# A decode kernel whose loads run on 16 DMA engines: part of one V unit moved to loads of 32 partitions, and the first K half issued ahead of wq

## The chip, the cores and the metric

One core of one Trainium2 chip runs the kernel. The metric is the device time of one execution in microseconds; quoted are medians of several executions. PE is the engine for matmuls (PEld its weight loads), DVE, ACT and POOL the vector, scalar and GpSimd engines, SP the one that issues the loads. SBUF is the memory on the chip that the loads fill, in tiles of 128 partitions; a DMA engine moves a load from HBM into it in packets, here one row of a partition or part of it each (the trace of the kernel before has 1920 packets of 16,384 bytes, 128 for each of the 15 units that are loaded whole). A ratio of two kernels is computed as the mean time of one kernel's fast runs over that of the other's in the same rounds, so it is not quite the ratio of the medians quoted beside it.

## The reference

A decode step for two tokens: layer norm, then attention over the last 2048 keys of a cache (32 query heads on 16 KV heads of 128), plus an MLP with squared ReLU, both added to the input. All tensors are bf16.

```python
xn = _layernorm(x)                                   # x: [2, 1, 576]
# attention: q = xn @ wq, window W = 2048 of 8192 keys, 16 KV heads, softmax, @ wo
# MLP: h = relu(xn @ w1 + b1) ** 2 ; h @ w2 + b2      (576 -> 4608 -> 576)
return x + attention(xn, k_cache, v_cache, wq, wo) + mlp(xn, w1, b1, w2, b2)
```

What matters for the time is that 53.6 MB of K, V and weights are read from HBM once, and little is computed on each byte.

## The kernel before

K and V come in eight units each (u = 0 to 7): 2 MB, a tile of 128 partitions with 16,384 bytes in each. A unit holds four heads of one batch; partition c*4 + h holds 64 keys of head h. V units and their pieces are written as `[c, h, bytes]`, c being the slowest dimension.

```python
TH = 4; CP = P // TH              # 4 heads x 32 chunks of 64 keys = 128 partitions
def unit_view(cache, u):
    tq, b = divmod(u, B)
    return cache[b, tq*TH:(tq+1)*TH, S0:Sk, :].rearrange("h (c j) d -> c h (j d)", c=CP)

def issue_kv(tiles, cache, u, name, parts=1):
    tl = kvpool.tile([P, UE], BF16, tag="kv", name=f"{name}_{u}")     # 6 buffers
    v = unit_view(cache, u); n = UE // parts; tiles[u] = tl
    return [lambda i=i: nc.sync.dma_start(out=tl[:, i*n:(i+1)*n], in_=v[:, :, i*n:(i+1)*n])
            for i in range(parts)]
# ... start: wq chunk 0, K half 0, wq chunk 1, K half 1, the rest of wq, then K1, w1, V0, ...
def load_v(u):
    for f in issue_kv(v_tiles, A_v_cache, u, "v"):
        f()
# ... end: w2 in five pieces, one after the other; out_ps gathers all products
W2P = [(0, 0, 9), (0, 9, 18), (1, 0, 9), (1, 9, 15), (1, 15, 18)]
```

Every large load covers 128 partitions. They are all issued on one queue (SP), most of them some 15 to 30 us before they land (medians of 13.0 to 29.4 us by the page, 6.9 for wq).

## Time and profile before

| | before |
|---|---|
| time | 137.48 us median of 3 |
| read from HBM | 53.6 MB, about 425 GB/s in the steady part |
| DMA engines | 90% busy or more in slices 2 to 38 of 40 |
| PE busy | 76% of the span, with waits for K units |
| last w2 piece complete | 132.26 us of a span of 135.6 |

Lines of the page of the kernel before: in the DMA line each digit is the busy share of one fortieth of the span (9 is 90% or more), below it what was moved; then a queue, and the shares of the chain of waits.

```profile
DMA  5999999999999999999999999999999999999940
GB/s 112 418 419 418 428 442 402 420 429 440 430 393 430 438 411 409 444 425 396 440 440 406 445 420 425 404 443 423 425 430 413 430 415 426 422 410 417 393 166 1
q8 instruction: 16, 0.26, 0.8%
DMA 55%; PE 35%; DVE 3%; issue 2%; POOL 1%; ACT 1%; SPq 1%; POOLq 0%; ACTq 0%
```

The rate stays at 393 to 445 GB/s in slices 2 to 38: the DMA engines do not run out of loads. The end of the chain of waits of the kernel before, in order of time (start, duration, what):

```profile
119.21 13.05 DMA w<-in_B_w_dram
132.26 0.04 issue
132.30 0.55 PE out_ps L213 x6
132.85 0.02 issue
132.87 0.45 DVE fin_sb L414
```

The last link is a load. PE's wait for K in the kernel before (in total, times, longest) has slack behind it, so PE is not what bounds the time:

```profile
PE kT_ps L237 <- DMA k<-in_A_k_cache_dram: 9.9, 4, 4.3
```

A load over 128 partitions adds to its semaphore (a counter on which other engines wait) 16 times, and PE goes on after the last: at 132.30 us, after 132.26. With 16 packets under way (in the trace of the kernel before exactly 16 at 216 of 236 moments, one every 0.5 us from 10 to 128 us), one increment is read here as one engine's. These 16 increments for the last w2 piece, in us, as the event records of the trace have them:

```
128.90 128.97 129.03 129.10 129.19 129.24 129.66 129.88
132.11 132.13 132.14 132.15 132.18 132.21 132.25 132.26
```

Eight engines are done about 3 us before the other eight, although the 128 packets of the piece all have 3456 bytes. The 16 packets of the instruction queue (q8), 16 KB each, tell why. They go with PE's program: 16 for some 4110 rows (the trace has 4108 weight loads and matmuls), and 8 for 2126 rows in fewer_pe_instructions below. The first of these fetches, at 16.75 us, took 1.06 us, an 8 KB data packet that starts as it ends took 0.81 us for 0.31, and from then on one increment of each load is about 1.45 us behind (25.87 us in K unit 1, whose other 15 come by 24.41). After eight fetches eight are; the ninth, at 79.6 us, puts one engine about 3 us behind (84.69 us in K unit 5, whose first seven increments come by 81.70).

### The profile page before, as it was taken

How to read it: one execution, taken by the hardware profiler on the slowest of the kernel's cores; microseconds unless marked ns; L12 is line 12 of the kernel's file. 1: busy time of each engine (PE TensorE's matmuls, PEld its weight loads, DVE VectorE, ACT ScalarE, POOL GpSimd, SP SyncE). 2: the span in 40 equal slices, each digit the busy share in tenths (PEclk: the TensorE clock that was granted, in tenths of full speed). 3: DMA queues.
4: the chain of work that ended last, by engine and by line, in shares of the span. 5: the costliest groups of instructions: out<-in, count | busy, mean ns of one | idle time of the engine just before them, and what ended most of it. 6: DMA issues, size and time to landing. Idle time of an engine off the chain costs nothing.

```text
span 135.6 us, 4461 instructions
## 1 busy us (share of the span) xinstructions
PE 102.5 (76%) x2054; PEld 91.9 (68%) x2054; DVE 53.9 (40%) x124; ACT 43.0 (32%) x47; POOL 10.0 (7%) x31
## 2 busy tenths in 40 slices
PE   1049947599968999879943993999399599768961
PEld 0039947589968999839933993688399479664530
DVE  7502421574352325422653446355634645660001
ACT  6705550165012521004701550272155127110000
POOL 6400000110110001100011001101100110110000
PEclk9999985569855685556985698698559959955599
DMA  5999999999999999999999999999999999999940
GB/s 112 418 419 418 428 442 402 420 429 440 430 393 430 438 411 409 444 425 396 440 440 406 445 420 425 404 443 423 425 430 413 430 415 426 422 410 417 393 166 1
DMA packets 5278, 53.90 MB, mean 397 GB/s; under 512 B 630, under 2 KB 652, under 8 KB 1164
## 3 DMA queue, kind: packets, MB, share of 16 engines
q1 hardware_dynamic: 5188, 53.61, 94.7%
q8 instruction: 16, 0.26, 0.8%
q0 software_dynamic: 64, 0.01, 0.0%
q14 instruction: 2, 0.02, 0.0%
q10 hardware_dynamic: 8, 0.00, 0.0%
HBM read 53.62 MB, written 0.00 MB: 395 GB/s over the span
## 4 chain that ended last, share of the span: by engine, by line
DMA 55%; PE 35%; DVE 3%; issue 2%; POOL 1%; ACT 1%; SPq 1%; POOLq 0%; ACTq 0%
DMA k<-in_A_k_cache_dram 41%; PE kT_ps L237 18%; DMA w<-in_B_w_dram 10%; PE hT_ps L323 5%; DMA b_sb<-in_B_b_dram 4%; PE sc_ps L252 4%; PE out_ps L213 4%; PE oT_ps L289 3%; PE qT_ps L225 1%; ACT kT L240 1%; POOL b_sb L146 1%; DVE l L271 1%; DVE sub L266 1%; SPq L94 0%; DVE fin_sb L414 0%
## 5 line engine op out<-in xcount | busy, mean ns | idle before, releaser
L237 PE MATMUL kT_ps<-ident,k 128*128 128x128 bf16 x512 | 47.3, 260 | 9.9 <-DMA k<-in_A_k_cache_dram 9.9
L237 PEld LDWEIGHTS <-k 128*128 128x128 bf16 x512 | 39.6, 119 | 11.8 <-DMA k<-in_A_k_cache_dram 10.7
L240 ACT COPY kT<-kT_ps 128x1024 bf16<-128x1024 bf16 x32 | 32.3, 1012 | 40.1 <-PE kT_ps L237 40.0
L242 DVE COPY kT<-kT_ps 128x1024 bf16<-128x1024 bf16 x32 | 22.0, 690 | 33.4 <-PE kT_ps L237 33.4
L252 PE MATMUL sc_ps<-qT_all,kT 128*128 128x8 bf16 x512 | 21.6, 168 | 1.6 <-ACT kT L240 0.8
L252 PEld LDWEIGHTS <-kT 128*128 128x128 bf16 x512 | 19.1, 100 | 2.6 <-ACT kT L240 1.2
L289 PE MATMUL oT_ps<-pT,v 128*128 128x8 bf16 x512 | 15.5, 167 | 1.9 <-issue 1.4
L269 ACT ACTIVATE pT<-sub 128x512 bf16<-128x512 f32 x8 | 5.0, 630 | 35.1 <-DVE sub L266 35.1
L289 PEld LDWEIGHTS <-v 128*128 128x128 bf16 x512 | 14.4, 99 | 2.1 <-issue 1.6
L271 DVE TENSOR_REDUCE l<-pT 128x8 f32<-128x512 bf16 x8 | 8.5, 1066 | 4.2 <-ACT pT L269 4.2
L213 PE MATMUL out_ps<-wo,ws 128*2 128x288 bf16 x64 | 8.3, 438 | 2.4 <-DVE ws L309 2.4
L323 PE MATMUL hT_ps<-xnT,w 128*128 128x2 bf16 x144 | 9.8, 201 | 0.0
L323 PEld LDWEIGHTS <-w 128*128 128x128 bf16 x144 | 9.4, 165 | 0.0
L258 DVE TENSOR_REDUCE m<-sc_ps 128x8 f32<-128x512 f32 x8 | 5.5, 692 | 9.7 <-PE sc_ps L252 9.7
L262 POOL PARTITION_ALL_REDUCE gmax<-m x8 | 2.9, 364 | 84.8 <-DVE m L260 84.8
L213 PE MATMUL out_ps<-w,hT_sb 128*2 128x288 bf16 x72 | 6.9, 353 | 1.3 <-DMA w<-in_B_w_dram 1.3
L213 PEld LDWEIGHTS <-ws 128*2 128x2 bf16 x64 | 3.5, 115 | 5.4 <-DVE ws L309 2.8
L213 PEld LDWEIGHTS <-hT_sb 128*2 128x2 bf16 x72 | 3.8, 103 | 4.3 <-issue 1.9
L266 DVE TENSOR_TENSOR sub<-sc_ps,gm 128x512 f32<-128x512 f32 x8 | 5.5, 692 | 0.3
L225 PE MATMUL qT_ps<-xnT,wq 128*128 128x2 bf16 x128 | 4.0, 165 | 2.2 <-DMA wq<-in_A_wq_dram 1.9
L225 PEld LDWEIGHTS <-wq 128*128 128x128 bf16 x128 | 3.9, 103 | 2.2 <-DMA wq<-in_A_wq_dram 2.0
L273 POOL PARTITION_ALL_REDUCE lsum<-l x8 | 3.2, 398 | 24.5 <-DVE l L271 24.5
(58 smaller groups left out, 35.1 us busy)
## 6 DMA issues: line engine op xcount, KB each, us to landing
v<-in_A_v_cache_dram SPq DMA_DIRECT2D x8, 2048.0 KB, 28.4
k<-in_A_k_cache_dram SPq DMA_DIRECT2D x7, 2048.0 KB, 29.4
w<-in_B_w_dram SPq DMA_DIRECT2D x4, 1152.0 KB, 17.7
wo<-in_A_wo_dram SPq DMA_DIRECT2D x4, 1152.0 KB, 27.4
wq<-in_A_wq_dram SPq DMA_DIRECT2D x4, 1024.0 KB, 6.9
w<-in_B_w_dram SPq DMA_DIRECT2D x3, 1296.0 KB, 22.7
k<-in_A_k_cache_dram SPq DMA_DIRECT2D x2, 1024.0 KB, 9.1
w<-in_B_w_dram SPq DMA_DIRECT2D x1, 864.0 KB, 15.7
```

The costliest lines, as they stand in the source:

```text
L213: nc.tensor.matmul(out_ps[32 * i:32 * i + B, :], lhsT=lhsT, rhs=rhs_of(i * OH, (i + 1) * OH), start=start, stop=stop, skip_group_check=True)
L225: nc.tensor.matmul(qT_ps[:, h, :], lhsT=lhsT, rhs=xnT[:, xc, :], start=(c == 0 and h == 0), stop=(c == KC - 1), skip_group_check=True)
L237: nc.tensor.transpose(out=kT_ps[:, i * P:(i + 1) * P], in_=k_sb[:, j * Dh:(j + 1) * Dh], identity=ident[:])
L240: nc.scalar.copy(out=kT[:], in_=kT_ps[:])
L242: nc.vector.tensor_copy(out=kT[:], in_=kT_ps[:])
L252: nc.tensor.matmul(sc_ps[:, g * JG + i, :], lhsT=kT[:, i * P:(i + 1) * P], rhs=qT_all[:, b, tq * NC:(tq + 1) * NC], start=True, stop=True)
L258: nc.vector.tensor_reduce(out=m1[:], in_=sc_ps[:].rearrange("p j c -> p c j"), axis=AX.X, op=ALU.max)
L266: nc.vector.tensor_tensor(out=sub[:], in0=sc_ps[:], in1=gm2[:].unsqueeze(1).to_broadcast([P, NJ, NC]), op=ALU.subtract)
L269: nc.scalar.activation(out=pT[:], in_=sub[:], func=ACT.Exp, scale=scale)
L271: nc.vector.tensor_reduce(out=l1[:], in_=pT[:].rearrange("p j c -> p c j"), axis=AX.X, op=ALU.add)
L289: nc.tensor.matmul(oT_ps[:], lhsT=v_sb[:, j * Dh:(j + 1) * Dh], rhs=pT_tiles[u][:, j, :], start=(j == 0), stop=(j == NJ - 1))
L323: nc.tensor.matmul(hT_ps[:, s * FR + r, :], lhsT=lhsT, rhs=xnT[:, xc, :], start=(c == 0 and s == 0 and r == 0), stop=(c == KC - 1), skip_g ...
```

## The change

The intent: give eight engines more of V unit 4 and eight less, so that all end together; and have K in earlier at the start.

```diff
     k0 = issue_kv(k_tiles, A_k_cache, 0, "k", parts=2)
+    k0[0]()
     issue_wq(0)
-    k0[0]()
+    k0[1]()
     issue_wq(1)
-    k0[1]()
...
+    SK = 43
+    SKU = NU // 2
     def load_v(u):
-        for f in issue_kv(v_tiles, A_v_cache, u, "v"):
-            f()
+        if u != SKU:
+            ...                                  # as before
+        tl = kvpool.tile([P, UE], BF16, tag="kv", name=f"v_{u}")
+        v_tiles[u] = tl
+        v = unit_view(A_v_cache, u)
+        e = (NJ - SK) * Dh                       # 5376 bytes of each partition
+        nc.sync.dma_start(out=tl[:, 0:e], in_=v[:, :, 0:e])
+        for c0, c1 in ((0, 16), (16, 24), (24, 32)):       # 11008 bytes of each
+            nc.sync.dma_start(out=tl[c0 * TH:c1 * TH, e:UE], in_=v[c0:c1, :, e:UE])
```

(Two dead statements also go.) So 64 partitions go in one piece and twice 32 in two pieces. In the trace of the changed kernel the piece of 64 partitions has 16 increments (85.72 to 92.32 us). Each piece of 32 has one increment about 1.2 us after its issue starts and eight more over the transfer (88.76 to 93.31 us for the first, 92.06 to 96.63 for the second), so it is taken to run on eight engines. "Lower", "low" or "lowest" below are the engines that carry loads of fewer than 64 partitions, "upper" the others. These are names only: no record numbers an engine or says which partitions it writes.

More of the change, by code (lines that the diff above doesn't have):

```diff
@@ L343, in load_k @@
             f()
+    SK = 43
+    SKU = NU // 2
     def load_v(u):
-        for f in issue_kv(v_tiles, A_v_cache, u, "v"):
-            f()
+        if u != SKU:
+            for f in issue_kv(v_tiles, A_v_cache, u, "v"):
+                f()
+            return
+        tl = kvpool.tile([P, UE], BF16, tag="kv", name=f"v_{u}")
[5 more added lines that the diff above has]
+            nc.sync.dma_start(out=tl[c0 * TH:c1 * TH, e:UE], in_=v[c0:c1, :, e:UE])
     W2P = [(0, 0, 9), (0, 9, 18), (1, 0, 9), (1, 9, 15), (1, 15, 18)]
@@ L360 @@
     load_k(3)
-    nxt = {0: [], 1: [], 2: [lambda: load_v(2), lambda: load_k(4)]}
     def step(u, extra=()):
@@ L404 @@
                 load_k(u + 2)
-        if u >= NU - 1:
-            pass
         if u == NU - 1:
```

## The prediction

> **What bounds the kernel.** The transfers. The page shows the 16 DMA engines at 90% busy or more in slices 2 to 38 of 40, 53.6 MB at about 425 GB/s; PE is busy 76% and idles before several K units (4.3 us before unit 5, 2.3 us before unit 6, in the timeline). The chain of waits is 55% DMA, and its last link is the landing of the last w2 piece (132.26 us), then six matmuls (0.53), one copy (0.45) and the output store.
>
> **Why engines could be unequal.** Every large transfer gives 16 engines the same bytes: 53.6 MB / 16 = 3.35 MB each, at 16 KB per 0.61 us. But the increments of the last w2 piece's completion (landing events in the trace) come in two groups: eight at 128.9 to 129.9 us, eight at 132.1 to 132.3. The packet records show why: 16 instruction packets of 16 KB, one about every 7.5 us. The first takes 1.06 us, and the next data packet on that engine 0.81 instead of 0.31; after it one landing is 1.45 us behind, after the second two, after the eighth eight; the ninth puts one engine about 3 us behind. So eight engines each serve two fetches and end about 2.7 us late, and each load waits for the slowest.
>
> **What the change does.** [...] The 32-partition pieces have eight chunks in front[...]. Of V unit 4, 64 partitions x 11,008 B (705 KB) move there: eight engines carry 44 KB more, the others 44 KB less, 1.64 us each way at 26.8 GB/s. Three issues are added (0.33 to 0.55 us each on SP, which issues over 20 us ahead) and 64 to 128 packets' overhead: under 0.1 us.
>
> If the late engines are the upper eight (records carry no engine number, so this is assumed from the intent), ends become: formerly early 128.9 to 129.9 plus 1.7 = 130.6 to 131.6; formerly late 132.2 minus 1.6 = 130.6. The last landing moves from 132.26 to between 130.8 and 131.6: 0.7 to 1.5 us saved. PE can follow: the K unit 6 landing that starts its final chain moves too, and PE idles 2.3 us before it.
>
> The K half ahead of wq: nothing. In PE order its transposes come behind the matmul on b2, which waits until 8.29 us; total bytes are equal, and PE is idle later anyway.
>
> **Risk.** [...] The three pieces each write one half, with other engines' work on it at once. [...] If the late engines are the lower eight, the time rises by 1.6 us (139)[...]. No trace here shows either.
>
> **Predicted: 136.5 us, range 135.7 to 138.0; faster by over 2%: 0.04, within: 0.92, slower: 0.04.**
>
> **Right if** the last piece's 16 increments lie within 1.2 us of one another (3.3 before), K unit 6 and everything behind it completes 0.7 to 1.5 us earlier, completions before V unit 4 hardly move, instruction fetches stay at 16, packet times of V unit 4 stay at 26 GB/s. **Wrong if** packets of V unit 4 or its neighbours stretch[...], if the two groups spread to 6 us (wrong half), or if the time falls over 2%: then the first K half mattered, seen as unit 0 work starting before 8 us.

## The result

The changed kernel took 145.08 us (median of 4, 144.94 to 146.17; a fifth execution of 144.48 us, which the ratio counts in), the kernel before 137.53 (median of 4): ratio 1.0555, 95% interval 1.05 to 1.061. It is slower by 5.5%, far outside the range. The profiled execution is the slowest of them, 146.17 us.

The same lines of the page of the changed kernel:

```profile
DMA  4999999999999999999999999999999999999600
GB/s 135 371 428 421 423 446 415 414 449 423 405 426 433 428 408 422 432 406 435 423 428 437 399 266 222 225 336 417 432 423 425 423 419 430 409 417 410 266 36 1
q8 instruction: 16, 0.26, 0.8%
DMA 72%; PE 20%; issue 1%; ACT 1%; DVE 1%; POOL 1%; SPq 1%; POOLq 0%; ACTq 0%
```

Nearly all of the loss is in one place. In four slices of 3.6 us the rate falls to 266, 222, 225 and 336 GB/s, while the busy line still shows nines: the page counts a DMA engine as busy while a packet is under way, however slowly (a DMA share of 1.00 at 219 GB/s from 88 to 92 us). Before and after that stretch the rate is the old one. The end of the chain of waits of the changed kernel:

```profile
125.71 14.80 DMA w<-in_B_w_dram
140.51 0.04 issue
140.55 0.55 PE out_ps L213 x6
141.10 0.02 issue
141.12 0.45 DVE fin_sb L423
```

It ends in the same way, 8.25 us later. And PE's waits in the changed kernel (how long in total, how often, the longest) follow the transfers: 14.1 us for K where it was 9.9, and a wait of its matmuls for V, for which before only one weight load waited, 0.6 us:

```profile
PE kT_ps L237 <- DMA k<-in_A_k_cache_dram: 14.1, 4, 6.0
PE oT_ps L289 <- DMA v<-in_A_v_cache_dram: 5.3, 2, 3.1
```

Packets of the trace say more. One of the 11,008-byte packets of V unit 4 takes 0.80 us at the median; the fastest take 0.42. They run from 82.5 to 95.5 us, 13 us in all. The increments of the last w2 piece:

```
133.45 133.51 135.09 135.72 136.12 136.14 136.16 136.28
136.35 136.37 136.77 136.81 136.88 137.76 139.28 140.51
```

They are spread over 7 us, for 3.4 before. So two things went wrong: throughput was lost, and the engines ended less equal than before. The second would delay the end even without the first, since the last engine counts.

### The profile page after: what moved, and what is told of

The parts are those of the page before. It is cut to its first block, busy times and chain, and to the rows that moved or that the text cites. A ratio compares the mean times of both kernels' runs of the same rounds, so it can differ in the third digit from the quotient of the medians.

```text
span 144.1 us, 4466 instructions
## 1 busy us (share of the span) xinstructions
PE 101.8 (71%) x2054; PEld 91.2 (63%) x2054; DVE 53.7 (37%) x124; ACT 43.0 (30%) x47; POOL 10.0 (7%) x31
## 4 chain that ended last, share of the span: by engine, by line
DMA 72%; PE 20%; issue 1%; ACT 1%; DVE 1%; POOL 1%; SPq 1%; POOLq 0%; ACTq 0%
DMA k<-in_A_k_cache_dram 58%; PE kT_ps L237 12%; DMA w<-in_B_w_dram 10%; DMA b_sb<-in_B_b_dram 4%; PE oT_ps L289 2%; PE sc_ps L252 2%; PE out_ps L213 2%; ACT kT L240 1%; PE qT_ps L225 1%; POOL b_sb L146 1%; DVE sub L266 0%; SPq L94 0%; DVE fin_sb L423 0%; POOL gmax L262 0%; SPq L100 0%
## 5 line engine op out<-in xcount | busy, mean ns | idle before, releaser
L237 PE MATMUL kT_ps<-ident,k 128*128 128x128 bf16 x512 | 47.8, 259 | 14.3 <-DMA k<-in_A_k_cache_dram 14.1
L213 PE MATMUL out_ps<-w,hT_sb 128*2 128x288 bf16 x72 | 6.4, 336 | 1.7 <-DMA w<-in_B_w_dram 1.7
```

The costliest lines, as they stand in the source:

```text
L213: nc.tensor.matmul(out_ps[32 * i:32 * i + B, :], lhsT=lhsT, rhs=rhs_of(i * OH, (i + 1) * OH), start=start, stop=stop, skip_group_check=True)
L237: nc.tensor.transpose(out=kT_ps[:, i * P:(i + 1) * P], in_=k_sb[:, j * Dh:(j + 1) * Dh], identity=ident[:])
```

## The experiments

Fifteen kernels ran. The first theory, P: the pieces write one half of the partitions at a time, and engines that write the same place slow each other. The mechanism was the author's assumption; no trace shows it. Rivals: the order at the start (O), the row sizes (R), the loads on eight engines as such (E). Edits are against the kernel before unless said otherwise; medians of the kernel before in the same rounds were 137.3 to 137.5 us.

### Each part of the change alone

`order_only` has the first hunk of the diff, `split_only` the second.

> Only the K half moves ahead of wq; V unit 4 loads as before. Theory P (the loss comes from the V pieces that write one half of the partitions[...]): the same as before within 0.4% (137.0 to 138.1 us). Rival O (the order costs part of the 7.6 us): 138.5 us or more.

> Only the pieces of V unit 4; the order of before. Theory P: all of the loss, 144.5 to 146 us. Rival O: clearly under 144 us.

Measured: order_only 137.60 us, ratio 1.0026 (1.0012 to 1.0041); split_only 145.64 us, ratio 1.0615 (1.058 to 1.065). The order is worth nothing, or 0.3% to the bad; the split is the whole loss. Three stretches of split_only show it (bounds and length in us, busy us of PE, PEld, DVE, ACT and POOL with their counts, then PE's clock, the DMA share and GB/s):

```profile
84.00:88.00 4.00, 3.41 (x30) 2.29 (x31) 1.80 (x4) 0.90 (x2) 0.40 (x1) 0.50 1.01 217
88.00:92.00 4.00, 4.00 (x76) 4.00 (x75) 1.77 (x3) 2.73 (x3) 0.00 (x0) 0.75 1.02 212
92.00:96.00 4.00, 2.05 (x65) 1.92 (x62) 2.28 (x6) 1.04 (x2) 0.36 (x1) 1.00 0.98 244
```

`columns_only` keeps the cut of the rows and drops the cut of the partitions:

```diff
-        for c0, c1 in ((0, 16), (16, 24), (24, 32)):
-            nc.sync.dma_start(out=tl[c0 * TH:c1 * TH, e:UE], in_=v[c0:c1, :, e:UE])
+        nc.sync.dma_start(out=tl[:, e:UE], in_=v[:, :, e:UE])      # 128 partitions
```

> V unit 4 in two loads of 5376 and 11008 bytes a row, both over all 128 partitions and 16 engines. Theory P: the same as before, 137.3 to 138.0 us, with packets of 11008 bytes near 0.42 us. Rival R (rows that are no power of two, or their HBM addresses, are slow): 140 us or more, with these packets near 0.7 us as in the changed kernel.

Measured: 137.40 us, ratio 1.0015 (0.9994 to 1.0036), packets of 11,008 bytes at 0.418 us. R falls, and 128 packets more hardly show (137.40 us for 137.36).

### No load on eight engines, yet slow

`halves_16_engines`: the pieces are `((0, 16), (16, 32))`, so 64 partitions each.

> The 11008-byte rows in two loads of 64 partitions (0 to 63, 64 to 127), each on 16 engines: no load on eight engines, and each engine moves the bytes of before. Theory P: [...]1.6 to 3.3 us lost: 139 to 141 us, with 11008-byte packets well over 0.42 us. Rival E (the loss comes from loads on eight engines, which overload the wrong eight): the same as before, 137.5 us.

Measured: 142.30 us, ratio 1.0346 (1.032 to 1.037), packets at 0.82 us, and the same stretches:

```profile
84.00:88.00 4.00, 3.64 (x37) 2.51 (x38) 1.62 (x5) 1.13 (x2) 0.40 (x1) 0.57 1.02 217
88.00:92.00 4.00, 3.81 (x93) 3.60 (x91) 2.04 (x3) 3.07 (x4) 0.00 (x0) 1.00 0.97 220
92.00:96.00 4.00, 2.41 (x89) 2.25 (x84) 2.41 (x5) 0.85 (x2) 0.36 (x1) 0.78 1.03 427
```

E falls as the whole cause; but the loss, 4.9 us, is over the 1.6 to 3.3 that P allowed.

`eight_own_half`: the mirrored pieces `((16, 32), (0, 8), (8, 16))`. The pieces of 32 partitions now go into partitions 0 to 63. P's number takes only the piece of 64 partitions to be slow; this was the author's assumption.

> The pieces of V unit 4 mirrored: partitions 64 to 127 in one load on 16 engines, partitions 0 to 31 and 32 to 63 on eight engines each, so that the eight engines move as many bytes as in the changed kernel[...]. Theory P: [...]about half of the 4.9 us that two such pieces cost: 138.5 to 140.5 us. Rival E (the overloaded eight engines cost the time, whatever they write): near the changed kernel, 144 us or more.

Measured: 142.81 us, ratio 1.040 (1.038 to 1.043). It beats the changed kernel, but misses what P said by over 2 us. Something in P is mis-sized; "Why the prediction was wrong" adds this run up.

### Which engines are late, and what does the place written cost

From here on the loads of the kernel stay as they were. Extra loads are added behind V unit 4 into a tile that nobody reads, all from the same addresses; only the partitions differ.

```diff
     def load_v(u):
         for f in issue_kv(v_tiles, A_v_cache, u, "v"):
             f()
+        if u == NU // 2:
+            v = unit_view(A_v_cache, u)
+            for p0 in (0, 32):                       # extra_low_x2; (0,) and (64, 96) in two others
+                nc.sync.dma_start(out=spare[p0:p0 + 32, :], in_=v[0:8, :, 0:XE])   # 11008 bytes
```

> The kernel before with one more load ahead of V unit 4's successors: 352 KB into partitions 0 to 31 of a tile that nobody reads, on eight engines, 44 KB or 1.64 us for each. If these eight are the early ones (2.4 to 3.3 us of slack at the end): no change, within 0.3%. If they are the late ones: 1.6 us more, 139 us.

> Two such loads, into partitions 0 to 31 and 32 to 63: 705 KB, 88 KB or 3.3 us for each of eight engines[...]. If they are the early ones: 0.1 to 1.2 us more than before (the slack is just used up). If the late ones: 3.3 us more, 140.7 us.

> The same two loads, from the same addresses[...], but into partitions 64 to 95 and 96 to 127. Theory P: [...]both groups lose 3.3 us or more: 141 to 144 us. Rival E (engines alone count): the same as with partitions 0 to 63 within 0.3%.

Measured: extra_low 138.97 us, ratio 1.0112 (1.010 to 1.013); extra_low_x2 140.98, 1.0269 (1.025 to 1.029); extra_high_x2 145.66, 1.0623 (1.058 to 1.067).

**The low eight are not simply early, nor simply late.** The increments of the last w2 piece in extra_low_x2:

```
128.90 129.68
131.99 131.99 132.01 132.06 132.10 132.19 132.20 132.23 132.37 132.65 132.85 133.30
135.07 135.17
```

Eight engines carry about 3.3 us more, and eight are about 3 us late by fetches. If these were the same eight, eight would stand near 129 and eight near 135.5; if they were the other eight, all would stand near 132.3. There are 2, 12 and 2: two engines have neither burden, twelve have one, two have both (12 + 2 x 2 = 16). So six of the eight late engines are outside the loaded eight, and two are inside. Those two make the time longer, by 1.6 us for 44 KB (extra_low) and 3.6 us for 88 KB. In extra_low the same reading would give 2, 6, 6 and 2 increments near 129, 130.7, 132.2 and 133.8, and they stand so: the last two at 133.55 and 133.90 us. By time alone both runs pass for the answer "late" (139 and 140.7 us); only the count of increments shows that two engines make it.

**The place written matters more.** The same bytes, in loads of the same shape, cost 3.6 us in partitions 0 to 63 and 8.3 us in 64 to 127. Two stretches of extra_low_x2:

```profile
88.00:92.00 4.00, 4.00 (x85) 3.96 (x84) 1.97 (x3) 2.44 (x4) 0.00 (x0) 0.83 1.03 433
92.00:96.00 4.00, 2.74 (x94) 2.51 (x90) 2.48 (x6) 0.85 (x2) 0.37 (x1) 1.00 1.00 420
```

And of extra_high_x2:

```profile
88.00:92.00 4.00, 4.00 (x84) 3.97 (x83) 1.99 (x3) 2.79 (x3) 0.00 (x0) 0.84 1.02 212
92.00:96.00 4.00, 3.06 (x104) 2.87 (x100) 2.31 (x6) 1.01 (x1) 0.36 (x1) 1.00 0.96 244
```

From 88 to 92 us the DMA share is the same (1.03 and 1.02) and the rate is half (433 and 212 GB/s). But P, with which only engines that write the same place slow each other, does not explain the packets: at 94.5 us only two of the extra packets are still under way, 14 engines are back at ordinary rows, and all 16 packets take nearly twice their time (9216-byte rows 0.64 to 0.73 us for 0.35). That gave a new theory, L: a few such writes hold back all 16 engines.

### Few engines

Loads of 16 or 8 partitions instead of 32 (`v[0:4]`, `v[0:2]`) run on four or two engines, 88 KB on each: of the eight increments of the last w2 piece that stood near 129 us, extra_low_4 leaves four there and extra_low_2 six.

> Two extra loads of 16 partitions each (0 to 15, 32 to 47), which four engines carry, 88 KB or 3.3 us each[...]. The earlier runs say that two of the eight late engines are among the lowest eight. If none of the two is among the lowest four: 137.3 to 138.2 us, with no increment of the last w2 piece over 0.8 us later than before. If one or two are: 140.5 to 141 us, with as many increments near 135.5 us.

> The same two loads into partitions 64 to 79 and 96 to 111[...]. Theory P[...]: eight engines slow, the other eight not; the rate falls to about 320 GB/s, never near 210. Theory L ([...]since in the run with eight engines the rate stayed near 210 GB/s when only two of the pieces' packets were left): the rate falls to near 210 GB/s, and most packets take twice their time, for 6.5 us or more; then 141 to 145 us.

> As with four engines, but 8 partitions each (0 to 7, 32 to 39), on two engines. None of the late ones among the lowest two: 137.2 to 138.0 us. One or two: 140.5 us and as many increments near 135.5 us.

> As with two engines, but into partitions 64 to 71 and 96 to 103[...], 177 KB in all. Theory P: four of 16 engines slow, rate about 370 GB/s, none of the other packets slow; about 140.5 us, since a late engine can be one of the four. Theory L: near 210 GB/s for 6.5 us or more, all packets slow; 140.5 to 144 us.

| run | partitions | engines, KB in all | us | ratio (95%) |
|---|---|---|---|---|
| extra_low_4 | 0-15, 32-47 | 4, 352 | 138.93 | 1.0104 (1.009 to 1.012) |
| extra_high_4 | 64-79, 96-111 | 4, 352 | 142.91 | 1.0394 (1.037 to 1.042) |
| extra_low_2 | 0-7, 32-39 | 2, 176 | 138.54 | 1.0075 (1.006 to 1.009) |
| extra_high_2 | 64-71, 96-103 | 2, 176 | 141.87 | 1.0319 (1.030 to 1.034) |

L holds for these places. The same stretches for extra_low_2, then for extra_high_2:

```profile
88.00:92.00 4.00, 4.00 (x71) 4.00 (x69) 1.38 (x2) 2.59 (x3) 0.00 (x0) 0.65 1.02 433
92.00:96.00 4.00, 3.71 (x119) 3.51 (x116) 2.28 (x5) 1.46 (x2) 0.36 (x1) 1.00 1.03 434
```

```profile
88.00:92.00 4.00, 4.00 (x91) 3.96 (x89) 1.73 (x3) 2.59 (x3) 0.00 (x0) 0.86 1.03 209
92.00:96.00 4.00, 2.48 (x89) 2.25 (x85) 2.48 (x6) 0.86 (x2) 0.37 (x1) 0.99 1.00 387
```

With P about 370 GB/s were expected; measured is 209. All 16 packets under way at 88 us, as bytes and duration in ns:

```
extra_low_2   9216: 347 347 348 348 348 348 348 348 348 348 348 355   11008: 413 413
              16384: 612 1091
extra_high_2  9216: 705 718 719 727 729 734   11008: 838 875
              16384: 1255 1271 1273 1274 1276 1281 1285 1444
```

And the number of engines that do it matters little: with two the loss is 4.4 us, with four 5.5. Read from the packets of each microsecond from 78 to 100 us, what was moved less than 425 GB/s adds up to 3.3, 3.5 and 4.6 us with two, four and eight engines (extra_high_x2), though the bytes double each time. The rest of the 8.3 us of extra_high_x2 is about what the same extra bytes cost in extra_low_x2, 3.6 us. The low runs miss what was expected (138.5 and 138.9 us for at most 138.0 and 138.2; in extra_low_4 the last increment is 1.15 us later than before, at 133.41 us, for at most 0.8). The extra bytes take more than the 3 us of slack that early engines have (88 KB at 16 KB in 0.61 us, as packets of the kernel before took, are 3.3 us, an estimate); that those engines are the last ones is assumed. No increment of either run stands near 135.5, and four and six stand near 129, so none of the four engines, and neither of the two, is late. If the four are among the eight that carry loads of 32 partitions, which is not shown, the two late ones of these are in the other four.

### The same two halves, at other partitions

Two loads of 8 partitions again, `p0 in (4, 36)` in extra_next_2: in partitions 0 to 63 as in extra_low_2, but four further on. Then `(72, 104)` in extra_cross_next_2: in 64 to 127 as in extra_high_2, but eight further on. For the first, one of two outcomes was expected, that of extra_high_2 or that of extra_low_2; for the second, that of extra_high_2 or about 400 GB/s with few slow packets.

> The two extra loads on two engines once more, but into partitions 4 to 11 and 36 to 43[...]. [...]the rate falls to near 210 GB/s for about 6.5 us, packets take twice their time, 141.5 to 142.2 us as with partitions 64 to 71. [...]no fall of the rate, 138.5 us as with partitions 0 to 7.

> The two extra loads on two engines, into partitions 72 to 79 and 104 to 111[...]. [...]near 210 GB/s for 6.5 us, all packets at twice their time, about 141.9 us. [...]

Measured: extra_next_2 141.45 us, ratio 1.0298 (1.028 to 1.032); extra_cross_next_2 141.97 us, ratio 1.0322 (1.030 to 1.035). The times are nearly equal, the ways to them are not. The stretch from 88 to 92 us of extra_next_2, and of extra_cross_next_2:

```profile
88.00:92.00 4.00, 4.00 (x93) 3.96 (x90) 1.73 (x4) 2.70 (x3) 0.00 (x0) 0.88 1.02 404
```

```profile
88.00:92.00 4.00, 4.00 (x79) 3.96 (x77) 1.81 (x3) 2.98 (x3) 0.00 (x0) 0.82 1.00 201
```

In extra_next_2 the rate falls by about a sixteenth (404 GB/s for 433 in extra_low_2). Of the packets at 88 us one of 9216 bytes takes 0.68 us and one of 11,008 takes 0.83, and the rest take their usual time. One increment of the last piece comes at 136.12 us and all others by 132.41: a single engine makes that time. That fits two engines that slow each other, as theory P has it; that they write the same place is not shown. So neither of the two outcomes came out whole. At 4 to 11 and 36 to 43 two packets of the 16 were slow, at 64 to 71 and 72 to 79 with their counterparts 32 further on the rate of all halved (209 and 201 GB/s). Why all engines slow down there is not shown.

### Are the fetches the reason that engines are late?

`fewer_pe_instructions` loads the same bytes and leaves out half of PE's program. Its output is wrong, which doesn't matter for the time. (The check did not notice what is left out.)

```diff
-        for i in range(JG):                          # scores: eight matmuls
-            nc.tensor.matmul(sc_ps[:, g * JG + i, :], lhsT=kT[:, i * P:(i + 1) * P], rhs=q, ...)
+        nc.tensor.matmul(sc_ps[:, g * JG:(g + 1) * JG, :], lhsT=kT[:, 0:P], rhs=q_broadcast, ...)
...                                                   # P V: one matmul of eight; q: two chunks of five
```

> Wrong on purpose: the loads of before, byte for byte, but half of the PE instructions (2126 rows for 4110; most P V and score matmuls left out). If instruction fetches make eight engines late: 7 or 8 fetches of 16 KB for 16, the late engines behind by one step (1.45 us) for two, the last w2 landing near 130.8 us for 132.26, and 135.5 to 136.4 us. If the late engines are slow of themselves: both groups 3 us apart as before, and within 0.4% of 137.4 us.

Measured: 136.03 us, ratio 0.9906 (0.989 to 0.992). Its line for the instruction queue:

```profile
q8 instruction: 8, 0.13, 0.4%
```

The increments of the last w2 piece are 128.88 to 129.98 (eight) and 130.41 to 130.78 (eight): the late eight are one step behind, not two. So the fetches make the lateness, and the second one on each engine costs this kernel 1.3 us. PE also did less in this run, but the span ends 3.3 us after the last increment, as before (134.1 us after 130.78, for 135.6 after 132.26), and the rate did not change (407, 432 and 430 GB/s in the stretches from 84 to 96 us, for 407, 437 and 422).

## Why the prediction was wrong

- **What bounds the kernel: right.** The transfers set the time in both kernels: the chain of waits ends on the last w2 piece, and the time moved with its last increment (8.25 us, for 8.5 us of the span, in the two profiled executions).
- **Two groups of eight engines, made by instruction fetches: right.** Half of the fetches (8 for 16) gave about half of the lag: the late eight end at 130.41 to 130.78 us for 132.11 to 132.26 (fewer_pe_instructions).
- **"If the late engines are the upper eight ... (assumed from the intent)": wrong.** Six are in the upper eight, two in the lower. The two got 44 KB more on top of their lag. This alone adds 1.6 us where 0.7 to 1.5 were to be saved: extra_low, which gives the eight the same 44 KB without slow writes, ended 1.6 us later. The prediction treated the choice as upper or lower, and both were wrong. The increments of the changed kernel, printed above, show the same count as extra_low_x2: two near 133.5 (neither burden), twelve from 135.1 to 137.8, two at 139.28 and 140.51 (both).
- **"Packet times of V unit 4 stay at 26 GB/s": wrong.** The 136.5 us rest on 11,008-byte packets at the usual rate (0.42 us); at the median they took 0.80. The loss of throughput was some 6 us. Every time that the prediction names was at least 4 us short. An estimate from the runs: the pieces' 1.41 MB at half of 425 GB/s would lose 3.3 us if all engines moved them at the same time. But in the few-engine runs the rate of all 16 halved while only two engines wrote in partitions 64 to 127 (209 GB/s in extra_high_2, 201 in extra_cross_next_2). So engines that come to the pieces at different times (the increments of the piece of 64 partitions lie between 85.72 and 92.32 us) would make it longer, which is the author's reading: the packets of the pieces last 13 us, most of it near half rate, where 1.41 MB at 217 GB/s would need 6.5.
- **The sum.** Adding up what split_only moved less than 425 GB/s in each microsecond from 78 to 100, read from the packets, gives 6.2 us; the two late engines add 1.6; together 7.8, and its last w2 piece came at 140.07 for 132.26, so 7.8 later. In halves_16_engines, where each engine's bytes stay equal, the same sum gives 4.4 us and the last piece is 4.4 us later; in eight_own_half it gives 3.1, with 1.6 for the late engines 4.7, and the last piece is 4.9 later. In the profiled execution of the changed kernel itself it gives only 5.7, with 1.6 then 7.3 of 8.25 us: some 0.9 us of this slowest execution stays open, of which 0.2 was lost before 78 us.
- **The chance of that risk was set too low.** Slower by over 2% was given 0.04, although no trace had shown how fast a load over half of the partitions runs, as the prediction itself says of its risks. The intent of the change was taken as a sign that it had found the right engines.
- **The K half ahead of wq does nothing: right**, within 0.3%. PE's first K transposes started at 8.60 us in the changed kernel, behind the matmul that waits for b2 until 8.27.
- The profile signs named in advance for this failure did appear: packets of V unit 4 and of its neighbours stretched, and the increments spread to 7 us. The spread is not that of its "wrong half", two groups 6 us apart: most increments lie in the middle.

No version that does the whole work beat the kernel before. Laying the moved bytes out in other partitions was not tried. An estimate from the runs: with the lag of 3 us between two groups of eight, perfect balance would save at most some 1.5 us.

## What to carry to other kernels

Read the rate, not only the busy share: in extra_high_2 the DMA share was 1.03 at 209 GB/s. If a transfer covers fewer than 128 partitions, read the rate while it runs, at more than one place: loads of the same 176 KB on two engines left 433 GB/s in partitions 0-7 and 32-39 (extra_low_2), 404 in 4-11 and 36-43 (extra_next_2), and 209 in 64-71 and 96-103 (extra_high_2). Before moving work from "late" to "early" engines, find out which ones are late with a spare load of a known size, and count the increments that move; and look at who is on them, here 16 fetches for the 4108 instructions of PE, each of which put one engine about 1.45 us behind.
